# Infini-attention and a tanhshrink feed-forward on one core: a third tile of P and of row maxima, beta planned instead of issued by hand, and a margin on the latencies of the planner

## The chip, the cores and the metric

The kernel runs on one core of a Trainium2 chip. Its time is the device time of one execution in microseconds, and smaller is better. A core has five engines that run side by side, each through its own list of instructions in order: PE (TensorE, the matrix array, whose weight loads are listed as PEld), DVE (VectorE), ACT (ScalarE), POOL (GpSimd) and SP (SyncE, which here only issues DMA transfers). They wait for one another by semaphores. PSUM is the memory that PE writes to, in banks; SBUF is the memory that all engines share.

## The reference

The first half is attention with a compressive memory, over 8 batches, 8 heads, 576 positions and 64 dimensions; the second is a feed-forward block on its 4608 x 512 result:

```
scores = q k^T / 8, causal;  a = softmax(scores);  local = a v
q_p = phi(q),  phi(x) = where(x > 0, x, exp(x) - 1) + 1
mem_out = (q_p M_prev) / (q_p . z_prev + 1e-6)
g = 1 / (1 + exp(-beta))                       # one number per head
x = g * mem_out + (1 - g) * local
out = (h - tanh(h)) @ w_out,  h = x @ w_in     # 512 -> 2048 -> 512
```

All inputs are float32; the kernel reads the two weight matrices as pairs of 32-bit words and decodes them on DVE.

## The kernel before

**Stages.** Attention goes head by head, 64 steps t (lines 1052 to 1121). In step t the scores of head t are made while the probabilities of head t - 1 are transposed and multiplied by V. Beside it, as work that fills PE, runs the first part of the feed-forward block, 6 of the 16 column chunks of `w_in` (`feed_a`, lines 1212 to 1241; its PSUM tiles are `psM`). When attention has been planned to its end, its memory is given back (line 1397), and the remaining 10 chunks are decoded into it and multiplied (`feed_b`, lines 1243 to 1384; PSUM tiles `psB`).

**One head.** `scores` (lines 900 to 939) multiplies q^T by k^T into a PSUM tile (`psS`, two banks, or `psA`), in three groups for the four query chunks. For each chunk DVE adds the causal mask, scales, writes the result into the SBUF tile `P` and the negated row maximum into `nm` (`masked`, line 333), and ACT takes the exponential in place and the row's sum (line 235). `P` and `nm` come from rings, lines 665 and 667: two tiles each before the change, given out in turn, so that head t + 2 writes where head t was. `scale_phi` (lines 941 to 960) takes 1 + exp(beta) (`eb`) into the row's sum and puts the memory's part of the row into `P` as well. `transp` (lines 962 to 981) transposes `P` on PE, and ACT and DVE copy the result to `pt` (for the first 6 head pairs to other tiles, `t` and `g`). `pv` (lines 989 to 1020) multiplies by V. The first 6 pairs (`EPV`, line 22) use plain float32 matmuls, the others a split into a rounded high part and the rest (`qx`, `kx`, `kz`, `vs`).

**Phi.** `prep_phi` (lines 807 to 822) makes phi(q) from q in natural layout (`qn`): two activations on ACT, a vector operation to `ph`, a product with `z` on POOL or DVE, a sum, and then `nr`, for which `enbx` = 1 + exp(-beta) is read (line 819).

**Before the plan.** Some instructions are issued by hand, in the order in which they stand (lines 703 to 734): the loads of the first pair's q^T on SP's queue and k^T on ACT's, the load of `beta` on ACT's queue (line 710), the mask and the identity on POOL, the copies of the mask and two exponentials of beta on ACT (lines 718 to 721), and on DVE four small instructions that make `eb`, `enbx` and `ebp` (lines 722 to 729). On ACT and DVE they so stand ahead of all planned work.

**The planner.** Everything else goes through `Plan` (line 104). A call like `pl.act` only notes an operation with its cost in ns, its engines and what it reads and writes. `run` (line 365) then simulates the engines: at each moment a free engine takes, among the operations that are ready, the one with the best rank. An operation is ready when those that it depends on have ended and `LAT` of their engine has passed (line 27; lines 458, 541 and 548); a PSUM bank is free `LAT` after its last user. A DMA's result counts as there 2000 ns after its end. From a first pass by priorities (`pl.pri`) follow four in all, each ranked by how late the pass before could have done an operation (`_latest`, line 402), so by the length of what hangs on it; the best is kept (lines 372 to 378). Then the instructions are given to each engine in the order of the plan. Engines start in it at the times of `START` (line 31). On the chip only the order counts; the engines wait for real semaphores.

**Fill.** To keep PE at work early, 44 matmuls on a tile of zeros (`zb`, line 738) stand at its head. Up to 60 us of planned time a gap in PE's plan is filled with more (line 384): gap less 60 ns, over 66 ns.

Of the kernel before, what the change touches and what calls it, by code (L numbers as in the profile page):

```python
# [9 lines left out]
F32 = mybir.dt.float32  # L10
# [3 lines left out]
AF = mybir.ActivationFunctionType  # L14
ALU = mybir.AluOpType
# [8 lines left out]
FCA = 6  # L24
PASSES = 4

LAT = {"PE": 200.0, "ACT": 150.0, "DVE": 130.0, "POOL": 150.0, "SP": 250.0}
FIRST = 44
FILL = 60e3

# [73 lines left out]
class Plan:  # L104
# [297 lines left out]
    def _latest(self, order):  # L402
# [33 lines left out]
        while left:  # L436
# [3 lines left out]
            for e in self.ENGINES:  # L440
                if free[e] <= now and heaps[e]:
# [13 lines left out]
                    for j in before[i]:  # L455
                        same = e == "PE" and eng[j] == "PE"
                        ready[j] = max(
                            ready[j], end + ops[j]["tail"] + (0.0 if same else LAT[eng[j]]))
                        need[j] -= 1
# [8 lines left out]
    def _schedule(self, todo, until, rank):  # L468
# [9 lines left out]
        for i in todo:  # L478
            d = [j for j in ops[i]["deps"] if ops[j]["end"] is None]
            need[i] = len(d)  # L480
            ready_at[i] = max(
                [ops[j]["end"] + LAT["SP"] for j in ops[i]["deps"] if ops[j]["end"] is not None],
                default=0.0,
# [10 lines left out]
        while len(done) < len(todo) and (until is None or left):  # L494
# [11 lines left out]
            for e in self.ENGINES:  # L506
# [4 lines left out]
                while h:  # L511
# [29 lines left out]
                    for x, pl in places:  # L541
                        x.left -= 1
                        if not x.left:
                            pl.user, pl.since = None, end + LAT[e]
                            heapq.heappush(wake, pl.since)
                    for j in succ.get(i, ()):
                        same = e == "PE" and ops[j]["opts"][0][0] == "PE"
                        ready_at[j] = max(ready_at[j], op["end"] + (0.0 if same else LAT[e]))
                        need[j] -= 1
# [19 lines left out]
def kernel(  # L569
# [11 lines left out]
    nc = tc.nc  # L581
# [3 lines left out]
    HP = H // 2  # L585
# [23 lines left out]
    att = att_ctx.enter_context(tc.tile_pool(name="att", bufs=1))  # L609
    ps_a = att_ctx.enter_context(tc.tile_pool(name="ps_a", bufs=1, space=PSUM))  # L610

    pl = Plan(nc)
# [14 lines left out]
    ident = const.tile([128, 128], F32, name="ident")  # L627
    mask = const.tile([128, S], F32, name="mask")
    mask0 = const.tile([128, HP, 64], F32, name="mask0")
    eb = const.tile([128, H], F32, name="eb")  # L630
    enb = const.tile([128, H], F32, name="enb")
    ebp = const.tile([128, HP], F32, name="ebp")
    enbx = const.tile([128, HP, 5, 2], F32, name="enbx")
    bt = const.tile([128, H], F32, name="bt")
# [27 lines left out]
    c0t = att.tile([128, HP, 128], F32, name="c0t")  # L662
    r_n0 = Ring(att, "n0", [128, 2, HP], F32, 2)
    r_xT = Ring(att, "xT", [128, 512], F32, 2)
    r_P = Ring(att, "P", [128, 1792], F32, 2)

    r_nm = Ring(att, "nm", [128, 12], F32, 2)
    r_rs = Ring(att, "rs", [128, 2, 4], F32, 2)
    rd = [dram.tile([2, 512], F32, name=f"rd{n}") for n in range(2)]
    r_tmp = Ring(att, "tmp", [128, 640], F32, 1)  # L670
# [35 lines left out]
    for h in range(2):  # L706
        a = slice(64 * h, 64 * h + 64)
        for w, e in ((0, nc.sync), (1, nc.scalar)):
            e.dma_start(out=r_qk.t[0][a, w], in_=qk[0, 0, a, w, h])
    nc.scalar.dma_start(out=bt, in_=beta.partition_broadcast(128))  # L710
    nc.gpsimd.memset(mask, 0.0)
    mf = mask[:, S - 128:S]
    nc.gpsimd.affine_select(
        out=mf, in_=mf, pattern=[[-1, 128]], compare_op=ALU.is_ge,
# [2 lines left out]
    make_identity(nc, ident)  # L717
    for a in (slice(0, 64), slice(64, 128)):
        nc.scalar.copy(mask0[a], mf[a, a].unsqueeze(1).broadcast_to([64, HP, 64]))
    nc.scalar.activation(out=eb, in_=bt, func=AF.Exp)  # L720
    nc.scalar.activation(out=enb, in_=bt, func=AF.Exp, scale=-1.0)
    nc.vector.tensor_scalar(
        out=eb, in0=eb, scalar1=1.0, scalar2=1e20, op0=ALU.add, op1=ALU.min)
    nc.vector.tensor_scalar(
        out=enbx, in0=enb.rearrange("p (a h) -> p a h", h=2).unsqueeze(2).broadcast_to(
            [128, HP, 5, 2]),
        scalar1=1.0, scalar2=None, op0=ALU.add)
    nc.vector.tensor_copy(ebp[0:64, :], eb[0:64, 0::2])
    nc.vector.tensor_copy(ebp[64:128, :], eb[64:128, 1::2])
    nc.gpsimd.memset(c0q, 0.0)  # L730
    for i in range(2):
        nc.gpsimd.memset(r_kz.t[i].bitcast(F32), 0.0)
    for t in (ident, mask, mask0, eb, ebp, enbx):
        pl.const.add(t.tensor.name)


# [21 lines left out]
    def load_qn(pr):  # L758
        b, p = divmod(pr, HP)
        d = prs.setdefault(pr, {})  # L760
        d["qn"] = r_qn.next()
        pl.dma(d["qn"], qn[b, p], False)
        zt[pr] = r_z.next()
        pl.dma(
            zt[pr], z_prev[b, 2 * p:2 * p + 2].rearrange("h d -> (h d)").partition_broadcast(128),
            False,
        )

    def load_qk(pr, w):
        b, p = divmod(pr, HP)  # L770
        d = prs.setdefault(pr, {})
        if pr < EPV:
            t = r_qk.next()
            d["qx"], d["kx"] = t[:, 0, 64:S], t[:, 1]
            for h in range(2 if pr else 0):
                a = slice(64 * h, 64 * h + 64)
                pl.dma(t[a], qk[b, p, a, :, h], False)
        else:
            d["raw"] = r_qk.next()
            pl.dma(d["raw"], qk[b, p, :, w], False)  # L780

    def load_v(pr):
        b, p = divmod(pr, HP)
        d = prs.setdefault(pr, {})
        if pr < EPV and (EPV - pr) % 2:
            d["vm"] = r_tmp.t[0].rearrange("p (c h d) -> p c h d", c=5, h=2)
        else:
            d["vm"] = r_vm.next()
        pl.dma(d["vm"], vm[b, p], False)
# [17 lines left out]
    def prep_phi(pr):  # L807
        p = pr % HP
        x = prs[pr]["qn"]
        e, ph, nr = r_e.next(), r_ph.next(), r_nr.next()  # L810
        pl.act(e, x, AF.Relu, scale=-1.0)
        pl.act(e, e, AF.Exp, scale=-1.0)
        pl.stt(ph, x, 0.0, e, ALU.max, ALU.add)
        pl.tt(
            e.rearrange("p c h d -> p c (h d)"), ph.rearrange("p c h d -> p c (h d)"),
            zt[pr].unsqueeze(1).broadcast_to([128, 5, 2 * D]), ALU.mult, "PV",
        )
        pl.red(nr, e, ALU.add)
        pl.stt(nr, nr, 1e-6, enbx[:, p], ALU.add, ALU.mult)
        pl.recip(nr, nr)  # L820
        d = prs.setdefault(pr, {})
        d["ph"], d["nr"] = ph, nr

    def prep_q(pr):
        d = prs.setdefault(pr, {})
        load_qk(pr, 0)
        if pr < EPV:
            return
        raw = d["raw"][:, :, 64:S]
        qx = d["qx"] = r_qx.next()  # L830
        pl.copy(qx, raw, "PAV")
        lo = slice(64, 128)
        pl.tt(qx[lo], raw[lo], qx[lo].bitcast(F32), ALU.subtract, "PV")
# [217 lines left out]

    def attention():
        pl.pri = -2.0
        prep_q(0)
        load_qn(0)
        pl.pri = 0.0
        prep_phi(0)
        load_v(0)
        load_c0(0)
        c0_phi(0)  # L1060
        load_qn(1)
        for t in range(2 * NPR + 1):
            pl.pri = float(t)
            pr, h = divmod(t, 2)
            act = t < 2 * NPR
            prv = t >= 1
            nxt = pr + 1 < NPR

            def at(key, f, *args):
                pl.pri = t + SH[key]  # L1070
                f(*args)

            order = ORD[h]
            if act:
                at('S', scores, t, order[0])
            if prv:
                at('T', transp, t - 1, 1)
                at('T', transp, t - 1, 2)
            if act:
                at('S', scores, t, order[1])  # L1080
                if h == 0 and pr % HP == HP - 1:
                    at('C', c0_trans, pr // HP)
            if prv:
                at('V', pv, t - 1, (1,))
                at('T', transp, t - 1, 3)
                at('V', pv, t - 1, (2,))
            if act:
                if h == 0 and pr % HP == HP - 1:
                    at('C', c0_out, pr // HP)
                at('S', scores, t, order[2])  # L1090
                at('N', scale_phi, t)
                if h:
                    at('N', turn_rs, pr)
            if prv:
                at('T', transp, t - 1, 0)
            if act and nxt:
                if h == 0:
                    at('P', prep_phi, pr + 1)
                    at('P', c0_phi, pr + 1)
                    at('P', prep_q, pr + 1)  # L1100
                else:
                    at('P', prep_k, pr + 1)
                    if pr + 2 < NPR:
                        at('L', load_qn, pr + 2)
            if prv:
                at('V', pv, t - 1, (3, 4, 0))
                if h == 0:
                    at('V', scale_x, pr - 1)
                    at('V', store_x, pr - 1)
            if act and nxt and h == 0:  # L1110
                if pr < EPV:
                    at('L', load_v, pr + 1)
                if pr + 1 >= EPV:
                    at('P', prep_v, pr + 1)
                    if pr + 2 < NPR:
                        at('L', load_v, pr + 2)
            if act and nxt and h == 1:
                if pr % HP == HP - 2:
                    at('C', c0_scores, pr // HP)
                if pr % HP == HP - 1:  # L1120
                    at('L', load_c0, pr // HP + 1)
# [366 lines left out]
```

## Time and profile before

| | us |
|---|---|
| three runs | 1195.31, 1202.38, 1201.07 |
| their median | 1201.07 |
| the profiled execution | 1203.01 |
| its span, first to last instruction | 1201.2 |
| mean granted TensorE clock in it | 0.989 |
| PE idle in the span (1201.2 - 1176.1) | 25.1 |

The profile is that of one execution. A busy PE is not PE at its peak, since matmuls overlap and their ends are modelled. The granted clock is the share of full speed that the chip let TensorE have. A wait is put down to the instruction that came last. Rows of a timeline give start, duration, engine, line, operation, tile written and tile read; "SPq" and "ACTq" mark the issue of a DMA transfer, not the transfer.

### The profile page before, as it was taken

To read this page: it belongs to the slowest core of one execution; us is meant where nothing else is said; L and a number is where in the kernel's file an instruction comes from. 1 tells how busy PE (TensorE), PEld (TensorE's weight loads), DVE (VectorE), ACT (ScalarE), POOL (GpSimd) and SP (SyncE) were. 2 spreads that over 40 slices of the span, in tenths; PEclk is the share of its full clock that TensorE was granted. 3 is DMA by queue.
4 is the path that set the end of the run, shared out by engine and by line. 5 is a ranking of instruction groups with operands and counts; after the bars stand their busy time and mean duration, and the time that the engine had idled before them with its cause. 6 is when DMAs were issued, how large, how long until landed. Compare 5 with 4: busy or idle time off the path is not lost. (4 is left out here: it accounts for less than half of the span.)

```text
span 1201.2 us, 20181 instructions
## 1 busy us (share of the span) xinstructions
PE 1176.1 (98%) x6899; PEld 1008.8 (84%) x6899; DVE 892.4 (74%) x2103; ACT 691.9 (58%) x1590; POOL 527.6 (44%) x580
## 2 busy tenths in 40 slices
PE   8999989999999999999999999999999999999998
PEld 4455878888898889889888888899898989889897
DVE  3767998898888887888875999893755739375571
ACT  4778986888788768777774565441322415142230
POOL 3566777888778866777670122020101102010110
PEclk7999999999999999999999999999999999999999
DMA  5566455455446354554412454312213031221101
GB/s 144 163 179 184 143 168 209 153 188 153 158 141 213 124 196 124 178 164 141 146 40 106 158 187 147 93 56 81 69 38 88 19 92 34 86 63 45 52 20 53
DMA packets 89831, 143.93 MB, mean 120 GB/s; under 512 B 20736, under 2 KB 54784, under 8 KB 89728
## 3 DMA queue, kind: packets, MB, share of 16 engines
q1 hardware_dynamic: 89424, 142.34, 37.9%
q8 instruction: 54, 0.88, 0.3%
q10 hardware_dynamic: 304, 0.30, 0.1%
q14 instruction: 49, 0.40, 0.1%
HBM read 114.17 MB, written 28.44 MB: 119 GB/s over the span
## 5 line engine op out<-in xcount | busy, mean ns | idle before, releaser
L203 PE MATMUL psB<-wi,ws 128*128 128x256 f32 x1620 | 210.1, 283 | 0.9 <-DVE t L271 0.7
L203 PEld LDWEIGHTS psB<-wi,ws 128*128 128x128 f32 x1620 | 203.9, 191 | 5.3 <-DVE ot L271 1.2
L203 PE MATMUL psM<-xh,wi 128*128 128x384 f32 x576 | 166.6, 349 | 1.8 <-DVE g L271 1.7
L235 ACT ACTIVATE P<-P,nm 128x576 f32<-128x576 f32 (+3 forms) x256 | 157.2, 617 | 19.4 <-DVE nm L333 18.5
L203 PE MATMUL psB<-woB,wo 128*128 128x512 f32 x612 | 148.9, 390 | 0.0
L211 PE MATMUL psA<-ident,P 128*128 128x128 f32 x886 | 143.6, 278 | 1.8 <-DVE pt L271 1.8
L203 PE MATMUL psM<-wo,gh 128*128 128x512 f32 x432 | 145.4, 402 | 0.0
L211 PEld LDWEIGHTS psA<-ident,P 128*128 128x128 f32 x886 | 106.8, 142 | 39.9 <-issue 11.5
L271 DVE TENSOR_TENSOR pt<-psA,pt 128x512 fp32r<-128x512 f32 (+1 forms) x208 | 124.9, 616 | 20.5 <-ACT pt L247 18.9
L271 DVE TENSOR_TENSOR ot<-psB,ot 128x256 f32<-128x256 f32 x225 | 87.7, 419 | 70.5 <-ACT ot L247 55.5
L203 PE MATMUL psA<-pt,vs 128*128 128x512 f32 (+3 forms) x520 | 129.8, 351 | 6.3 <-DVE pt L271 4.5
L203 PEld LDWEIGHTS psB<-woB,wo 128*128 128x128 f32 x612 | 112.8, 188 | 22.0 <-DVE wo L271 0.2
L247 ACT CAST pt<-psA 128x512 fp32r<-128x512 f32 (+1 forms) x208 | 107.5, 532 | 40.4 <-PE psA L211 38.2
L203 PEld LDWEIGHTS psM<-xh,wi 128*128 128x128 f32 x576 | 105.2, 190 | 6.3 <-DVE g L271 3.4
L203 PEld LDWEIGHTS psA<-pt,vs 128*128 128x128 f32 x520 | 87.6, 193 | 16.7 <-DVE pt L271 6.1
L203 PE MATMUL psM<-xl,wi 128*128 128x384 f32 x288 | 99.4, 345 | 0.0
L247 ACT COPY ot<-psB 128x256 f32<-128x256 f32 x22 | 8.2, 374 | 154.6 <-PE psB L203 153.4
L276 POOL TENSOR_TENSOR P<-ph,nm 128x128 f32<-128x128 f32 x128 | 67.2, 544 | 62.7 <-DVE nm L271 30.7
L203 PEld LDWEIGHTS psM<-wo,gh 128*128 128x128 f32 x432 | 79.1, 188 | 13.1 <-DVE g L271 0.3
L271 DVE TENSOR_TENSOR rawB<-psB,xh 128x512 f32<-128x512 f32 x34 | 23.3, 689 | 88.5 <-PE psB L203 88.4
L333 DVE CUSTOM_DVE_ANT_0 P<-psA,mask 128x320 f32<-128x320 f32 (+2 forms) x160 | 69.5, 458 | 25.7 <-PE psA L203 20.1
L333 DVE CUSTOM_DVE_ANT_0 P<-psS,mask 128x576 f32<-128x576 f32 (+1 forms) x96 | 67.8, 706 | 26.0 <-PE psS L203 21.0
(226 smaller groups left out, 2619.3 us busy)
## 6 DMA issues: line engine op xcount, KB each, us to landing
qk<-in_qk_dram SPq DMA_DIRECT2D x52, 576.0 KB
qn<-in_qn_dram SPq DMA_DIRECT2D x32, 320.0 KB
vm<-in_vm_dram SPq DMA_DIRECT2D x29, 320.0 KB
xh<-part SPq DMA_DIRECT2D x36, 256.0 KB
out_dram<-rawB SPq DMA_DIRECT2D x36, 256.0 KB
xr<-xs SPq DMA_DIRECT2D x11, 768.0 KB
part<-ot SPq DMA_DIRECT2D x11, 768.0 KB
e<-rd SPq DMA_DIRECT2D x64, 128.0 KB
```

The source lines that it names most:

```text
L203: [("PE", max(109.0, n * c / 2.4 + 13), lambda: nc.tensor.matmul(real(out), lhsT, rhs, start=start, stop=stop, **kw))],
L211: [("PE", self._n(out) * 2 / 2.4 + 3, lambda: nc.tensor.transpose(real(out), in_, ident))],
L235: [("ACT", c, lambda: nc.scalar.activation(out=out, in_=real(in_), func=func, **kw))],
L247: "ACT", n / 1.2 + (51 if ps else 93), lambda: nc.scalar.copy(out, real(in_))
L271: lambda: nc.vector.tensor_tensor(out=out, in0=real(a), in1=b, op=op),
L276: lambda: nc.gpsimd.tensor_tensor(out=out, in0=a, in1=b, op=op),
L333: [("DVE", self._n(out) / 0.96 + 115, lambda: nc.vector.tensor_tensor_reduce(out=real(out), in0=real(in_), in1=mask, scale=-scale, scalar= ...
```

## The change

Three parts. The rings of P and of row maxima get a third tile each. The load of beta moves from ACT's queue to SP's and becomes a planned operation, the first that is noted, with the priority of the first loads of q (-2); the two exponentials and four DVE instructions on it are planned too, and `eb`, `enbx` and `ebp` are marked as constant after that. And `LAT` rises by 200 ns for PE, ACT, DVE and POOL; SP's stays.

```diff
-LAT = {"PE": 200.0, "ACT": 150.0, "DVE": 130.0, "POOL": 150.0, "SP": 250.0}
+LAT = {"PE": 400.0, "ACT": 350.0, "DVE": 330.0, "POOL": 350.0, "SP": 250.0}
...
-    r_P = Ring(att, "P", [128, 1792], F32, 2)
-
-    r_nm = Ring(att, "nm", [128, 12], F32, 2)
+    r_P = Ring(att, "P", [128, 1792], F32, 3)
+
+    r_nm = Ring(att, "nm", [128, 12], F32, 3)
...
-    nc.scalar.dma_start(out=bt, in_=beta.partition_broadcast(128))
...
-    nc.scalar.activation(out=eb, in_=bt, func=AF.Exp)
-    nc.scalar.activation(out=enb, in_=bt, func=AF.Exp, scale=-1.0)
-    nc.vector.tensor_scalar(
-        out=eb, in0=eb, scalar1=1.0, scalar2=1e20, op0=ALU.add, op1=ALU.min)
-    nc.vector.tensor_scalar(
-        out=enbx, in0=enb.rearrange("p (a h) -> p a h", h=2).unsqueeze(2).broadcast_to(
-            [128, HP, 5, 2]),
-        scalar1=1.0, scalar2=None, op0=ALU.add)
-    nc.vector.tensor_copy(ebp[0:64, :], eb[0:64, 0::2])
-    nc.vector.tensor_copy(ebp[64:128, :], eb[64:128, 1::2])
...
-    for t in (ident, mask, mask0, eb, ebp, enbx):
+    for t in (ident, mask, mask0):
         pl.const.add(t.tensor.name)
...
     def attention():
         pl.pri = -2.0
+        pl.dma(bt, beta.partition_broadcast(128), False)
+        pl.act(eb, bt, AF.Exp)
+        pl.act(enb, bt, AF.Exp, scale=-1.0)
+        pl.ts(eb, eb, 1.0, 1e20, ALU.add, ALU.min)
+        pl.ts(
+            enbx, enb.rearrange("p (a h) -> p a h", h=2).unsqueeze(2).broadcast_to([128, HP, 5, 2]),
+            1.0, None, ALU.add, None)
+        pl.copy(ebp[0:64, :], eb[0:64, 0::2], "V")
+        pl.copy(ebp[64:128, :], eb[64:128, 1::2], "V")
+        for t in (eb, ebp, enbx):
+            pl.const.add(t.tensor.name)
         prep_q(0)
         load_qn(0)
```

## The prediction

> **What bounds the kernel now.** I read the page first, then the stretches table (busy time of each engine by stage), then the opening in order of time, then the waits of attention.
>
> ```profile
> span 1201.2 us, 20181 instructions
> PE 1176.1 (98%) x6899; PEld 1008.8 (84%) x6899; DVE 892.4 (74%) x2103; ACT 691.9 (58%) x1590; POOL 527.6 (44%) x580
> ```
>
> TensorE has work in 1176.1 of 1201.2 us. The profiled execution took 1203.0 us with its span of 1201.2, so 1.8 lie outside. What the change can win is idle time of PE, 25.1 us, and what a lower granted clock costs. The stretches table says where both lie (columns: stretch, its length, PE, PEld, DVE, ACT, POOL busy with counts, granted clock, DMA share, GB/s):
>
> ```profile
> 0.00:8.30 8.30, 7.32 (x53) 6.37 (x54) 0.11 (x1) 2.09 (x3) 4.19 (x11) 1.00 0.56 131
> 8.30:10.40 2.10, 0.03 (x1) 0.06 (x1) 0.00 (x0) 0.00 (x0) 0.00 (x0) 0.91 0.58 189
> 10.40:12.30 1.90, 0.00 (x0) 0.00 (x0) 1.34 (x7) 1.60 (x5) 0.00 (x0) 0.50 0.82 297
> 12.30:27.50 15.20, 15.19 (x34) 6.71 (x33) 8.62 (x29) 7.96 (x22) 3.41 (x5) 0.51 0.52 132
> 30.00:120.00 90.00, 90.00 (x368) 45.34 (x368) 62.26 (x173) 70.01 (x170) 55.56 (x63) 1.00 0.60 175
> 120.00:630.00 510.00, 495.90 (x3013) 439.78 (x3012) 433.50 (x1053) 403.97 (x960) 389.86 (x421) 0.99 0.49 155
> 630.00:720.00 90.00, 88.56 (x453) 78.68 (x453) 76.59 (x165) 50.80 (x107) 13.57 (x9) 1.00 0.45 150
> 750.00:1201.20 451.20, 447.46 (x2781) 404.45 (x2779) 279.00 (x619) 138.28 (x294) 51.02 (x66) 1.00 0.20 59
> ```
>
> Three places. The opening: PE empty from 8.3 to 12.3 us, then half clock until 27.5. Attention proper, 120 to 630: 510.0 - 495.9 = 14.1 us idle, and a clock of 0.99. The end from 750 on is full but for 3.7 us, most of it the drain of the last block, which no part of the change touches. So the second half is not where I look for a gain.
>
> The opening in order of time (start, duration, engine, line, what; in brackets the idle time before and its releaser):
>
> ```profile
> 0.98 4.98 PE L738 MATMUL psS<-zb 128*128 128x128 bf16 x45 [0.98 <-DVE zb L704]
> 1.99 0.58 SPq L348 DMA_DIRECT2D qn<-in_qn_dram  x1
> 2.25 0.62 ACTq L710 DMA_DIRECT2D bt<-in_beta_dram  x1
> 2.62 0.43 SPq L348 DMA_DIRECT2D z<-in_z_prev_dram  x1
> 5.89 1.57 PE L203 MATMUL psS<-qk 64*128 64x288 f32 x4
> 10.67 0.21 ACT L720 ACTIVATE eb<-bt 128x8 f32<-128x8 f32 x1 [5.66 <-DMA bt<-in_beta_dram]
> 10.89 0.72 ACT L235 ACTIVATE e<-qn 128x640 f32<-128x640 f32 x1
> 10.91 0.17 DVE L722 TENSOR_SCALAR eb<-eb 128x8 f32<-128x8 f32 x1 [9.98 <-ACT eb L720]
> 11.49 0.76 DVE L333 CUSTOM_DVE_ANT_0 P<-psS,mask 128x576 f32<-128x576 f32 x1
> 12.29 0.78 ACT L235 ACTIVATE P<-P,nm 128x576 f32<-128x576 f32 x1
> 12.31 0.27 PE L738 MATMUL psS<-zb 128*128 128x128 bf16 x1 [3.98 <-DVE nm L333]
> 14.51 2.07 PE L203 MATMUL psA<-qk 64*128 64x192 f32 x4
> 15.29 0.67 ACT L235 ACTIVATE P<-P,nm 128x448 f32<-128x448 f32 x1 [1.14 <-DVE nm L333]
> 16.52 0.69 PE L211 MATMUL psA<-ident,P 128*128 128x128 f32 x2
> ```
>
> Beta's 4 KB land at 10.67, 8.4 us after their issue. ACT and DVE run in order, and both have what is made of beta at their heads. The first scores are in PSUM at 5.89 + 1.57 = 7.46, but DVE's first masked maximum starts at 11.49, because four small instructions on beta stand before it. PE needs that PSUM bank again and waits 3.98 us.
>
> **The change, part by part.** Durations are from rows; the planner's own costs I use for the order of work alone.
>
> (1) Beta. Gone from the head: ACT's DMA issue (0.62), two exponentials (0.21 for the first) and four DVE instructions (10.91 to 11.49, 0.58 together). All come back as planned work, so nothing is saved by their removal, only by their place. The first masked maximum is then free at about 7.5 instead of 11.49. The next PE instruction followed that start by 12.31 - 11.49 = 0.82, so it comes at 8.3, and the 3.98 us gap closes. The issue moves to SP. The planner's ranks put first what has the longest chain behind it: q's natural tile feeds two 640-wide activations and three wide vector operations before it meets what beta gives, which has one 8-wide activation and one small vector operation; so I expect q first and beta second or third. z, the first weight block and V, behind it, are issued up to 0.62 later; z is first read by POOL after a 640-wide vector operation that hasn't begun at 12.31, so that is covered; uncovered it would be 0.62. Beta will hardly land before 10. What stands behind it on ACT is then the exponential of the first scores (12.29 now), on DVE the fourth masked maximum, no longer the first. Late next, in that order: q's tile for ACT, and head 0's exponentials, for which PE's first transposes (16.52) wait.
>
> What that is worth. If q lands only just before 10.89, the first exponential of scores stays at 12.29, but the last of the four no longer waits 1.14 for a PE slowed behind the gap: transposes about 1.4 earlier. At best the whole gap is won on top, 1.4 + 4.0 = 5.4, because head 1's scores (2.07 us and more, after 14.51) fit into the wait. I take 3.5, about the middle, and keep 0 to 5.4, 0 for the case that beta lands later than now.
>
> The half clock from 10.4 to 27.5 is a second price: 15.2 us of PE work at about 0.51 would be 7.6 shorter at full clock. I don't take it. The rows of attention say why:
>
> ```profile
> 190.94:194.35 3.41, 1.76 (x8) 0.87 (x6) 3.31 (x7) 3.38 (x9) 3.41 (x5) 1.00 0.28 43
> 194.35:197.77 3.42, 3.42 (x11) 2.93 (x12) 2.88 (x8) 1.69 (x7) 2.08 (x3) 0.50 0.88 362
> 324.06:327.47 3.41, 1.37 (x9) 1.11 (x7) 3.35 (x4) 0.85 (x2) 3.41 (x3) 1.00 0.52 159
> 327.47:330.90 3.43, 3.43 (x13) 2.96 (x14) 3.31 (x10) 1.99 (x5) 1.95 (x2) 0.50 0.62 183
> 443.40:446.77 3.37, 1.57 (x9) 1.22 (x9) 3.34 (x6) 0.72 (x2) 0.63 (x1) 1.00 0.30 76
> 446.77:450.20 3.43, 3.43 (x13) 3.19 (x12) 1.39 (x7) 0.85 (x3) 3.10 (x6) 0.52 0.52 175
> ```
>
> Three times a stretch of 3.4 us in which PE was busy 1.4 to 1.8 us was followed by one at half clock. In the new opening PE has the rest of head 0's scores and head 1's to do between 8.3 and about 12, then waits for exponentials until about 14: again a stretch that is about half busy. So the drop more likely moves than goes.
>
> [...]
>
> (2) The margin of 200 ns on the four compute engines' hops. It adds no instruction but fill matmuls: fills are planned gap less 60, over 66 ns, so before head 0's third score group one becomes about seven. 45 of them took 4.98 us, 0.11 each, so 0.7 us there, in time in which PE else idles; without that cover the same few groups would cost 1 to 2. It lies inside the 0 to 5.4 above. Otherwise it changes the order on every engine: PE is planned to do another head's or the feed-forward's work for 200 ns more before it meets a result. What it can win is in these rows:
>
> ```profile
> PE psA L203 <- DVE pt L271: 4.5, 4, 2.0
> PE psA L211 <- DVE pt L271: 1.8, 5, 0.7
> PE psA L203 <- DVE nm L333: 1.5, 2, 1.2
> DVE P L333 <- PE psA L211: 5.2, 12, 1.0
> L271 DVE TENSOR_TENSOR qx<-qk,qx x16: 1214/1222/3607, 127.7 to 588.5; 64x1024 fp32r<-64x1024 f32 x16
> ```
>
> (From 120 to 630: waits with total us, times, longest; the last row has minimum, median and maximum ns.) PE's waits for `pt` are nine of 0.7 us on average, (4.5 + 1.8) / 9; two or three hops lie between a transpose and the product that needs it, 0.4 to 0.6 us of new slack. So I take half of the 14.1 us, 7.0, and one clock drop of three, 0.5 x 3.42 = 1.7: about 8.5. Ends: all of it, 14.1 + 3 x 1.7 = 19; and a loss, since a new order also places new collisions: three more stalls like those above (1.6 to 2.0 idle and 1.7 of clock) cost about 11, which the lost order of (3) below rounds to 12.
>
> (3) Third tiles of P and of row maxima. They remove DVE's wait for the transposes that free P, the 5.2 us in 12 above. DVE has 510.0 - 433.5 = 76.5 us idle there, so alone this is worth nothing on the path; it lets the margin's earlier scores start. They cost only memory. Cover gone, it is at most 5.2.
>
> Sum: 1203.0 - 3.5 - 8.5 = **1191.0**. The median of the three runs, 1201.07, is 1.9 below the profiled execution and the runs spread over 7; I make no correction and count the difference into the range.
>
> **The rivals.**
>
> *The opening keeps its clock.* If the fills and head 1's scores keep PE more than about half busy until the transposes, the 7.6 come on top: 1203.0 - 3.5 - 7.6 - 8.5 = **1183.4**. For it: six fills more per gap, a gap of 4 us less. Against it: the three pairs of rows above.
>
> *The margin is too small for what it meets.* The three drops coincide with DVE subtractions of `qx` that took up to 3.607 us against a median of 1.222; 2.4 us is not met by 0.2 per hop. Then attention stays and only the opening counts: 1203.0 - 3.5 = **1199.5**. For it: long stalls hold much of the 14.1. Against it: most waits for `pt` are shorter than 1 us. [...]
>
> *Attention becomes longer than its cover (slower).* Larger latencies make the planner slip a feed-forward matmul in front of attention work that is in truth ready. One per head, at 15.0 / 81 = 0.185 us (row below), over 64 heads is 11.8. Attention then ends 11.8 later, and so begins the decoding of the second half's weights, which needs attention's memory and fills DVE:
>
> ```profile
> 690.00:705.00 15.00, 15.00 (x81) 14.04 (x80) 15.00 (x35) 9.30 (x20) 0.00 (x0) 1.00 0.48 160
> ```
>
> The matmuls that cover it between 630 and 720 were spent early, so PE idles that long: 1203.0 - 3.5 + 11.8 = **1211.3**. It decides as soon as the matmuls left at attention's end last less than the decoding, and now they end about when it does: PE 88.56 of 90 from 630 to 720. Against it: only if PE's extra matmuls delay attention and don't fill its 14.1 idle.
>
> **How the numbers follow.** Forecast 0.38, kept clock 0.24, margin too small 0.25, slower attention 0.13. About 1% (12 us: below 1189 or above 1213) is what a measurement of this kernel tells from no change. Faster by more: nine tenths of the kept clock (0.22), four tenths of the forecast (0.15), little else: 0.38. Slower by more: half of the last rival, whose 1211.3 is near the border (0.07), and a bad end of the attention term otherwise (0.03): 0.10. Within: 0.52. The range must reach the kept clock at 1183.4 with some of the attention term's upper half, and the third rival with a few lost microseconds, and leave out most of the last: 1179 to 1208.
>
> **What would show it.** Right: the first masked maximum at about 7.5, beta's issue on SP behind q's natural tile, no PE gap of 4 us before 12; PE idle from 120 to 630 near 7 and two drops instead of three; the wait of masked maxima for transposes all but gone. The half clock beginning one or two stretches later, at 13.8 or 17, is the forecast; none before 30 is the first rival. Wrong: idle of 14 or more in attention with the qx maximum unchanged (margin too small), or psM matmuls ended long before the first psB ones, with PE idle between (slower).

## The result and the profile after

The changed kernel takes 1177.26 us (median of four runs, 1175.71 to 1178.65); the kernel before took 1198.57 beside it (four runs, 1195.31 to 1202.38). The ratio is 0.9838, with a 95% interval of 0.98 to 0.9876. The forecast of 1191.0 had the direction and, against 1201.07, half of the size (0.8% of 1.6%); the time in us lies 1.7 below the low end of its range, 1179 (as a share, 1179 of 1201.07 is 0.9816, and the measured ratio lies above it). The profiled execution took 1178.65, its span is 1176.8.

First the stretches table of the changed kernel:

```profile
8.30:10.40 2.10, 2.10 (x14) 1.24 (x13) 1.88 (x7) 1.69 (x6) 0.00 (x0) 1.00 0.91 312
...
12.30:27.50 15.20, 14.94 (x65) 7.39 (x63) 11.52 (x40) 11.32 (x31) 6.29 (x9) 1.00 0.85 191
120.00:630.00 510.00, 500.71 (x3090) 454.61 (x3090) 433.88 (x1051) 404.19 (x961) 385.23 (x419) 1.00 0.51 157
630.00:720.00 90.00, 88.03 (x465) 78.05 (x464) 88.40 (x191) 46.37 (x98) 11.05 (x11) 0.98 0.48 152
```

PE is no longer empty from 8.3 on, and the clock stays full from 12.3 to 27.5, where it was 0.51: 65 matmuls instead of 34. From 120 to 630 PE idles 9.3 us instead of 14.1. The opening in order of time:

```profile
2.24 0.60 SPq L348 DMA_DIRECT2D qn<-in_qn_dram  x1
...
2.88 0.43 SPq L348 DMA_DIRECT2D bt<-in_beta_dram  x1
3.36 0.51 SPq L348 DMA_DIRECT2D z<-in_z_prev_dram  x1
...
6.34 0.74 ACT L235 ACTIVATE e<-qn 128x640 f32<-128x640 f32 x1 [2.27 <-DMA qn<-in_qn_dram]
...
7.11 0.21 ACT L235 ACTIVATE enb<-bt 128x8 f32<-128x8 f32 x1
...
7.34 0.76 DVE L333 CUSTOM_DVE_ANT_0 P<-psS,mask 128x576 f32<-128x576 f32 x1 [6.41 <-PE psS L203]
...
8.14 0.78 ACT L235 ACTIVATE P<-P,nm 128x576 f32<-128x576 f32 x1
...
8.64 1.02 PE L203 MATMUL psS<-qk 64*128 64x448 f32 x2
...
8.88 0.82 DVE L315 SCALAR_TENSOR_TENSOR ph<-qn,e 128x640 f32<-128x640 f32 x1
...
10.52 1.55 POOL L276 TENSOR_TENSOR e<-ph,z 128x640 f32<-128x640 f32 x1 [5.66 <-DMA z<-in_z_prev_dram]
...
10.86 0.44 PE L211 MATMUL psA<-ident,P 128*128 128x128 f32 x2
```

Beta is second in SP's queue, behind q's natural tile. Both had landed when ACT could use them, q at 6.34 and beta by 7.11 (no bracket, so no wait). The first masked maximum starts at 7.34, and the first transposes at 10.86, 5.7 us earlier than before.

To see where the time came from, I cut each profiled execution at two starts: the last product of the six early head pairs with V out of `t` (the PE row below), and the last sum into `xT`, which ends attention (the DVE row). Rows by tile give them (minimum, median, maximum ns; first and last start). Before:

```profile
L271 DVE TENSOR_TENSOR xT<-psA,tmp x52: 621/689/696, 148.3 to 644.0; 64x512 f32<-64x512 f32 x52
L203 PE MATMUL psA<-t,tmp x24: 592/592/644, 42.9 to 132.7; 128*64 128x512 f32 x24
```

After:

```profile
L271 DVE TENSOR_TENSOR xT<-psA,tmp x52: 621/690/696, 134.0 to 619.6; 64x512 f32<-64x512 f32 x52
L203 PE MATMUL psA<-t,tmp x24: 592/593/643, 36.2 to 122.8; 128*64 128x512 f32 x24
```

So the early pairs end at 122.8 instead of 132.7 (9.9 less), attention from there takes 619.6 - 122.8 = 496.8 instead of 511.3 (14.5 less), and the rest 1176.8 - 619.6 = 557.2, as before (1201.2 - 644.0 = 557.2). Together 24.4, the difference of the spans. The medians differ by 21.3: the profiled execution lies 4.4 above the median before and 1.4 after.

The stretches table of the middle part alone, before and after:

```profile
132.70:644.00 511.30, 497.77 (x3022) 443.06 (x3021) 427.22 (x1037) 399.21 (x949) 382.14 (x414) 0.99 0.48 152
```

```profile
122.80:619.60 496.80, 487.51 (x3017) 442.56 (x3016) 424.66 (x1029) 398.62 (x948) 382.11 (x416) 1.00 0.50 155
```

Only 4.2 of the 14.5 are idle time of PE (511.3 - 497.8 = 13.5 became 9.3). The other 10.3 lie in its busy time, with almost the same number of matmuls. Some 3.4 of these are clock, by my estimate, since two stretches of 3.4 us at half clock are gone (0.50 from 402.0 to 405.4 is the one left; before there were three, at 0.50, 0.50 and 0.52); about 6.9 are time in which PE reads as busy at full clock on the same work.

### The profile page after: what moved, and what is told of

Its sections match the earlier page's. It is cut to its first block, busy times and chain, and to the rows that moved or that the text cites. A ratio compares the mean times of both kernels' runs of the same rounds, so it can differ in the third digit from the quotient of the medians.

```text
span 1176.8 us, 20151 instructions
## 1 busy us (share of the span) xinstructions
PE 1160.3 (99%) x6907; PEld 1005.3 (85%) x6907; DVE 904.3 (77%) x2133; ACT 673.4 (57%) x1565; POOL 516.2 (44%) x575
## 5 line engine op out<-in xcount | busy, mean ns | idle before, releaser
L203 PE MATMUL psB<-wi,ws 128*128 128x256 f32 x1620 | 212.5, 284 | 2.0 <-DVE ot L271 1.6
L235 ACT ACTIVATE P<-P,nm 128x320 f32<-128x320 f32 (+3 forms) x256 | 156.8, 615 | 9.6 <-DVE nm L333 8.8
L203 PE MATMUL psB<-woB,wo 128*128 128x512 f32 x612 | 153.3, 391 | 0.0
L211 PE MATMUL psA<-ident,P 128*128 128x128 f32 x883 | 140.6, 276 | 6.3 <-DVE pt L271 5.2
L247 ACT COPY ot<-psB 128x256 f32<-128x256 f32 x44 | 16.4, 372 | 148.8 <-PE psB L203 143.0
L203 PE MATMUL psM<-wo,gl 128*128 128x512 f32 x216 | 86.3, 402 | 0.0
L276 POOL TENSOR_TENSOR P<-ph,nm 128x128 f32<-128x128 f32 x128 | 63.9, 518 | 45.1 <-DVE nm L271 29.7
```

The source lines that it names most:

```text
L203: [("PE", max(109.0, n * c / 2.4 + 13), lambda: nc.tensor.matmul(real(out), lhsT, rhs, start=start, stop=stop, **kw))],
L211: [("PE", self._n(out) * 2 / 2.4 + 3, lambda: nc.tensor.transpose(real(out), in_, ident))],
L235: [("ACT", c, lambda: nc.scalar.activation(out=out, in_=real(in_), func=func, **kw))],
L247: "ACT", n / 1.2 + (51 if ps else 93), lambda: nc.scalar.copy(out, real(in_))
L276: lambda: nc.gpsimd.tensor_tensor(out=out, in0=a, in1=b, op=op),
```

## The experiments

My theory after the result: beta's place gives the early part, by an earlier start and by the clock; the margin gives attention; the third tile gives nothing by itself. Rivals: the clock is kept by the fill that the margin plans; the margin needs the third tile; the shorter attention is only the luck of a new order. The third tiles with the old latencies have no plan at all (the planner comes to a point where nothing is ready and nothing ends), so "without margin" beside three tiles is a margin of 10 ns.

The cuts of all profiled executions, by the same two rows, and the times with their ratio to the kernel before, run beside them ("PE busy" is PE's busy time within attention). Each cut is of one execution: e5's took 1198.3, where its median is 1203.4.

| kernel | early pairs | attention | PE busy | rest | median | ratio (interval) |
|---|---|---|---|---|---|---|
| before | 132.7 | 511.3 | 497.8 | 557.2 | 1198.6 | |
| changed | 122.8 | 496.8 | 487.5 | 557.2 | 1177.3 | 0.9838 (0.98 to 0.9876) |
| e1 beta | 121.9 | 508.7 | 497.0 | 557.5 | 1190.2 | 0.9915 (0.9895 to 0.9936) |
| e2 margin | 136.1 | 497.8 | 488.1 | 562.0 | 1196.1 | 0.9959 (0.993 to 0.9988) |
| e3 tiles | 130.2 | 504.4 | 494.6 | 559.8 | 1194.5 | 0.9943 (0.9921 to 0.9965) |
| e4 fill | 131.4 | 508.1 | 494.7 | 557.4 | 1197.3 | 0.9969 (0.9946 to 0.9991) |
| e5 margin, tiles | 129.1 | 506.7 | 488.8 | 560.7 | 1203.4 | 1.0023 (1.0002 to 1.0043) |
| e6 beta, margin | 126.7 | 503.0 | 487.5 | 561.9 | 1195.5 | 0.9974 (0.9956 to 0.9993) |
| e7 beta, tiles | 124.3 | 509.9 | 495.6 | 560.3 | 1192.4 | 0.9936 (0.9914 to 0.9957) |
| e8 fill, other bank | 125.4 | 508.4 | 494.8 | 556.9 | 1192.3 | 0.9932 (0.9915 to 0.9949) |
| e9 190 ns | 122.0 | 494.5 | 487.2 | 559.6 | 1180.5 | 0.9851 (0.9825 to 0.9877) |
| e10 210 ns | 127.0 | 503.9 | 488.7 | 554.4 | 1185.1 | 0.9886 (0.9851 to 0.992) |
| e11 300 ns | 122.6 | 495.0 | 487.5 | 559.2 | 1178.1 | 0.9825 (0.9808 to 0.9843) |
| e12 100 ns | 121.5 | 507.2 | 490.5 | 557.1 | 1190.9 | 0.9932 (0.9909 to 0.9956) |

**e1, beta alone.**

```diff
 # the changed kernel, with
+LAT = {"PE": 200.0, "ACT": 150.0, "DVE": 130.0, "POOL": 150.0, "SP": 250.0}
+    r_P = Ring(att, "P", [128, 1792], F32, 2)
+    r_nm = Ring(att, "nm", [128, 12], F32, 2)
```

> Beta planned, with two tiles of P and the old latencies. If the opening's gain is beta's place alone: first masked maximum near 7.4 us, no PE gap of 4 us, full clock from 7 to 27, and 11 us less than the kernel before, about 1188, with attention as uneven as before (idle from 120 to 630 near 14 us). If the opening keeps its clock only because the margin plans more fill: the half clock comes back at 10 to 17 us, and the time is only about 4 us less, 1195.

The first branch, with 9.3 us less. Its stretches:

```profile
8.30:10.40 2.10, 1.99 (x9) 0.98 (x9) 2.10 (x9) 2.10 (x8) 0.00 (x0) 1.00 0.86 281
...
12.30:27.50 15.20, 15.07 (x62) 6.96 (x61) 12.41 (x38) 11.78 (x29) 6.13 (x9) 1.00 0.74 178
120.00:630.00 510.00, 498.30 (x3038) 444.99 (x3037) 427.06 (x1046) 398.06 (x958) 395.38 (x421) 0.99 0.49 153
```

The clock is full without the margin's fill, so the fill isn't what keeps it here. Attention is nearly as long as before (508.7), with 11.7 us of PE's time idle from 120 to 630.

The clock isn't safe in every execution, though. In e7 (below), also with beta planned and without the margin's fill, beta landed later, and DVE had to make `enbx` of it ahead of head 0's next masked maximum, for which PE waited. The stretch that follows (clock 0.78) lost, by my estimate, about 0.22 x 15.2 = 3.3 us:

```profile
9.29 0.21 ACT L235 ACTIVATE enb<-bt 128x8 f32<-128x8 f32 x1 [2.04 <-DMA bt<-in_beta_dram]
...
9.54 0.18 DVE L291 TENSOR_SCALAR enbx<-enb 128x40 f32<-128x40 f32 x1 [1.27 <-ACT enb L235]
9.63 0.35 DVE L333 CUSTOM_DVE_ANT_0 P<-psA,mask 128x192 f32<-128x192 f32 x1
...
10.46 1.13 PE L203 MATMUL psA<-qk 64*128 64x192 f32 x4 [0.76 <-DVE nm L333]
```

```profile
12.30:27.50 15.20, 15.20 (x48) 6.57 (x47) 9.38 (x32) 10.14 (x28) 4.15 (x8) 0.78 0.62 155
```

The other seven traces with beta planned, e1's among them, read 1.00 there. Whether the margin's fill would have saved e7's is open.

**e2, the margin alone.** Only the line of `LAT` is the changed kernel's.

> The margin alone: beta at the head as before, two tiles of P. If margin and beta are worth their own stretch each: opening as before (gap near 4 us, half clock for about 17), attention 13 us shorter, about 1186. If the margin needs the third tile of P, since heads planned further apart run into the ring: attention no shorter than before, 1199 or more. If the gain in attention is only the luck of a new order: anything from 1190 to 1205.

Attention is 13.5 shorter (497.8 of 511.3), as the first branch said and without a third tile. The time is not: the early part is 3.4 longer than before (136.1), and behind attention 4.8 us are given back (rest 562.0). There, from 630 to 760, PE waits for DVE's sums out of `psB`, a wait that the kernel before doesn't have:

```profile
PE psB L203 <- DVE ot L271: 4.2, 4, 2.4
```

Its ten runs differ by 14 us, and the granted clock goes with them; five of the ten:

```
us        1185.41  1187.15  1194.11  1196.26  1199.76
clock       1.000    0.997    0.991    0.988    0.989
```

By its clock of 0.989 I estimate that the slowest run lost 0.011 x 1199.76 = 13.2 us; the run at full clock is 14.4 faster.

**e3, the third tiles alone**, the kernel before with three tiles and 10 ns.

> The third tiles alone, with a margin of 10 ns instead of 200. If the ring is off the path: within 4 us of the kernel before, 1195 to 1203, and the wait of masked maxima for PE's transposes falls. If the ring is what makes attention shorter: about 1186, with idle from 120 to 630 below 10 us.

1194.5, just below the first branch; PE's idle time from 120 to 630, 9.8 us, is that of the second, but not its time. Attention is 6.9 shorter, but the wait of masked maxima for transposes is 4.9 us in 8 where it was 5.2 in 12, so that wait isn't the reason.

**e4 and e8, the kernel before with PE kept at work.** e4 puts 76 matmuls on zeros where one stood, e8 72 into another bank:

```diff
+                if pe is not None and n and not self.filled:
+                    n, self.filled = 0, True
+                    for _ in range(72):
+                        self.idle(other=True)
                 for _ in range(n):
                     self.idle()
...
+    def idle(first=False, other=False):
+        to = bM[1].tile[:, 0:128] if other else bS[0].tile[:, 832:960]
+        nc.tensor.matmul(to, zb, zb, start=first or other, stop=False, skip_group_check=True)
```

> The kernel before with 76 matmuls on zeros instead of one behind the first scores, where PE waits for beta; beta stays where it is. If the half clock that follows is what the wait costs most: full clock up to 27 us and beyond, about 7 us less, 1191, though DVE begins no earlier than 11.5. If the cost is the late start itself: no less than 2 us are won, 1197 or more.

e4 missed its own point. The zeros go to the tile whose scores wait for DVE, so they wait too, and then stand in the way:

```profile
11.54 6.47 PE L741 MATMUL psS<-zb 128*128 128x128 bf16 x76 [3.63 <-DVE nm L334]
```

> The kernel before, with 72 matmuls on zeros into a PSUM bank that nothing else uses at that time, behind the first scores, where PE waits for beta; beta stays at the head. PE is then busy from 8.3 to about 12.3. If PE's idle time is what halves the clock, and the clock lost is time lost one for one: clock share near 0.997 instead of 0.992, 6 to 7 us less than before, about 1193. If the clock falls for another reason (little work in the matmuls of the first heads): half clock from 13 on all the same and within 2 us of before.

e8 does fill the wait, and 7.4 us are won:

```profile
8.30:10.40 2.10, 2.10 (x42) 2.10 (x40) 1.81 (x9) 1.11 (x4) 0.00 (x0) 1.00 1.00 334
...
12.30:27.50 15.20, 15.20 (x64) 7.29 (x62) 11.67 (x35) 11.87 (x31) 6.66 (x9) 1.00 0.54 140
```

The same work on beta at the head, and a full clock: the early pairs end 7.3 earlier (125.4). Beta landed earlier as well, at 8.30 instead of 10.67. But PE's next scores, which here stand behind the zeros, start only 0.5 earlier than in the kernel before (first row e8, second row before), so about 6.8 of the 7.3 are clock:

```profile
11.99 1.02 PE L204 MATMUL psS<-qk 64*128 64x448 f32 x2
```

```profile
12.51 1.86 PE L203 MATMUL psS<-qk 64*128 64x448 f32 x2
```

e1, where DVE also starts earlier (7.79 instead of 9.12), has 121.9. The 3.5 between them are that start or the other order; one pair can't tell. In the kernel before, the half clock lasted through 15.2 us in which PE reads as busy (0.51 from 12.3 to 27.5), where a drop in attention was one stretch (0.50 from 194.35 to 197.77), by my estimate 0.5 x 3.42 = 1.7 us; for the opening the two traces say about 6.8.

**e5, e6, e7: one part taken back.** e5 has beta at the head again, e6 two tiles, e7 a margin of 10 ns.

> The changed kernel with beta's load, exponentials and vector instructions back at the head: margin and third tiles alone. If each part is worth its own stretch: opening with a gap of 2 to 4 us and a half clock of 17 us, attention as short as in the changed kernel; about 10 us over it, 1187 to 1189. If margin and third tile are worth only what each alone was (3.4 and 5.0 of 1199.5): 1191. If a third tile is what the margin needs: clearly less than 1191.

> The changed kernel with two tiles of P and of row maxima: beta and margin alone. If the parts add up: 1199.5 less 9.3 for beta and 3.4 for the margin, 1187. If the margin needs the third tile: no better than beta alone, 1190 or more. If the ring is off the path: 1177, as the changed kernel.

> The changed kernel with a margin of 10 ns in place of 200: beta and third tiles alone. If the parts add up: 1199.5 less 9.3 for beta and 5.0 for the tiles, 1185. If the margin is what shortens attention: 1190, as beta alone. If any new order is as good as the margin: 1177 to 1180.

e6 and e7 went their middle branches in time: each is no better than beta alone, so the parts do not add up run by run. e5 missed all of its figures. Its ten runs have clocks from 0.988 to 0.994, so part of its 1203 is clock; and PE idles 17.9 us in its attention (506.7 - 488.8), more than in the kernel before. Why, no run shows. In the cuts the three lie between the kernel before and the changed one: attention 506.7 and 503.0 with the margin, 509.9 without.

**e9 to e12: other margins**, 190, 210, 300 and 100 ns in the changed kernel.

> The changed kernel with a margin of 190 ns instead of 200. If the margin as such shortens attention: within 2 us of the changed kernel, 1175 to 1179, and nearly its order. If the order that came out of 200 is a lucky one among many: another order, attention 3 to 12 us longer, 1180 to 1192.

> The same with 210 ns. Margin as such: 1175 to 1179. Lucky order: 1180 to 1192, and not the same time as with 190.

> The same with 300 ns. If more slack goes on helping: 1177 or less. If the slack is paid for where weights of the second half are decoded (margin and third tiles alone had PE idle there): 630 to 750 us with PE below 116 of 120 and 1182 or more. Lucky order: 1180 to 1192.

> The same with 100 ns. If the margin works by its size: between no margin (1192.4 with 10 ns) and the changed kernel (1177.3), about 1185. Lucky order: no relation, anything from 1177 to 1195.

Ten ns less or more make another order, with 494.5 and 503.9 us of attention: so there is luck, about 5 us to either side. But it has a centre. The seven kernels with 190 ns or more have 494.5 to 506.7, 499.7 in the mean; the four orders with 10 ns or none have 504.4 to 511.3, 508.6 in the mean (e4 and e8 have the order of before). The margin is worth 8.9 us there, in the mean.

PE's busy time in attention shows it more clearly, for it doesn't overlap: 487.2 to 488.8 in the seven with 190 ns or more, 494.6 to 497.8 in the four with 10 ns or none, with 3001 to 3035 matmuls in all of them. That is 8.3 of the 8.9. Clock alone doesn't make it: e7 and e9 both read a clock of 1.00 from 120 to 630, and have 495.6 and 487.2. PE's idle time, attention less busy time, does overlap, 7.3 to 17.9 and 9.8 to 14.3: that is where one order differs from another. With 100 ns attention is as long as without a margin (507.2), but PE's busy time, 490.5, has already fallen most of the way, and 16.7 us of idle time hide it.

Two tiles or three make no difference that stands out: 497.8 and 503.0 with two and the margin. e11 came between its first two branches: no more is won with 300, and PE is busy 116.6 of 120 us from 630 to 750. The waits there show best in e9:

```profile
690.00:705.00 15.00, 9.62 (x60) 9.05 (x60) 14.51 (x29) 5.46 (x12) 10.98 (x3) 0.84 0.52 157
```

```profile
700.46 0.68 DVE L315 SCALAR_TENSOR_TENSOR mask<-rawB,mask 128x512 int32<-128x512 int32 x1
701.06 0.41 DVE L252 COPY ot<-psB 128x256 f32<-128x256 f32 x1
701.40 1.07 DVE L271 TENSOR_TENSOR ot<-psB,ot 128x256 f32<-128x256 f32 x3
...
701.95 2.90 PE L203 MATMUL psB<-wi,ws 128*128 128x256 f32 x12 [5.38 <-DVE ot L271]
```

PE has 5.4 us idle and loses clock (0.84), while DVE is busy 14.51 of 15 us. PE waits for sums that DVE takes out of `psB`, and they stand in DVE's order behind the decoding of weights (`rawB`). That attention's earlier end (616.5, 27.5 us before that of the kernel before) puts the decoding there is likely, but not shown.

No kernel beats the changed one beyond the noise: e11 has the lowest ratio, and its interval overlaps the changed kernel's.

## Why the prediction was half right

*What bounds the kernel*: right. All of the gain lies before attention's end; the rest is 557.2 in both.

*(1) Beta, the earlier start, 3.5*: one pair agrees in size (e1 against e8: 3.5), but the eight orders with beta planned differ by 5.5 among themselves (121.5 to 127.0), so that isn't shown. The order in SP's queue, q, beta, z, was right.

*(1) The clock*: the step that failed. I priced it at 7.6 and didn't take it, since "the drop more likely moves than goes". It is about 6.8 in e8, and it went. Under that sentence stood two wrong landings: "Beta will hardly land before 10", and q's natural tile put as late as 10.89. They came by 7.11 and at 6.34, so the first transposes started at 10.86 and not at about 14, and the half-busy stretch that I laid out between never came. What the forecast feared does exist: e7, where beta landed at 9.29, lost 3.3 us of clock. The rival that keeps its clock named what came (1.00 from 12.3 to 27.5), and its 1183.4 is the nearest of the four figures; of its two reasons the gap mattered, and the fills were not needed in e1.

*(1) What is displaced*: z held POOL up, but only from the end of `ph` at 8.88 + 0.82 = 9.70 to 10.52, 0.8 us; the 5.66 in its row are all of POOL's idle time. No PE wait follows from it, so that cover held.

*(2) The margin, 8.5*: near the mean over orders (8.9), too small for this order (14.5), and near the mean by luck. I took 7.0 from PE's idle time and 1.7 from the clock, and put its busy time at nothing. In the changed kernel idle time gave 4.2, the clock 3.4 and the rest of the busy time 6.9; in the mean, idle time gave 0.6 and busy time 8.3. PE's own waits for `pt` did not shrink: 4.5 + 1.8 in nine became 5.2 + 1.4 in five. What went are its waits for row maxima, of which the matmuls' view has no row left (1.5 on `psA` and 1.3 on `psS` before), and most waits of the weight loads, which run beside the matmuls. Theirs before, from 120 to 630 (total us, times, longest):

```profile
PEld psA L203 <- DVE pt L271: 6.2, 7, 2.3
...
PEld psA L203 <- DVE nm L333: 2.4, 3, 1.6
PEld psS L203 <- DVE nm L333: 2.3, 4, 1.8
```

The same view of the changed kernel:

```profile
PEld psA L203 <- DVE pt L271: 1.6, 1, 1.6
...
PEld psA L203 <- DVE nm L333: 0.2, 1, 0.2
```

and its matmuls' waits for `pt`:

```profile
PE psA L211 <- DVE pt L271: 5.2, 4, 2.1
...
PE psA L203 <- DVE pt L271: 1.4, 1, 1.4
```

The products' loads for `pt` go from 6.2 to 1.6 and those for row maxima from 4.7 to 0.2. All rows of that view add up to 33.7 us in 72 waits before and 16.2 in 23 after; over the kernels it is 53 to 72 waits without the margin and 23 to 46 with it. Many short waits gone, a few long ones left: that fits a slack of 200 ns. That these waits are the busy time that went is argued, not shown. The rival "too small" saw its cause rightly: the one half clock left in attention, at 402 us, follows a subtraction of `qx` that took 2.55 us and a wait of PE of 2.11 us, and by the rows by tile another still takes 3.711; why some take that long, no run shows:

```profile
L271 DVE TENSOR_TENSOR qx<-qk,qx x13: 1222/1224/3711, 131.2 to 565.4; 64x1024 fp32r<-64x1024 f32 x13
```

But most of what could be won lay elsewhere. The clock fell once in attention instead of three times; I had taken one drop gone.

*(3) The tiles, nothing alone*: not refuted, though e3 is 5 us faster than before; 504.4 of attention is within what a new order does. That their wait would be all but gone was wrong: from 120 to 630 it is

```profile
DVE P L333 <- PE psA L211: 4.3, 7, 1.4
```

after 5.2 in 12. What they do bring in one order or another stays open: two tiles and three can't be planned in the same order.

*The slower rival* asked for attention longer than its cover. Attention became shorter, and PE still came to wait beside the decoding: 1.6 us at 699 in the changed kernel, 5.4 in e9, each time for DVE's sums out of `psB`. That is a place to look at next.

In sum, beta's place is worth 8.4 in the early part (mean of eight kernels with it, 123.6, against four with it at the head and no added fill, 132.0) and the margin 8.9 in attention: 17.3 of the 24.4. Of the other 7, 3.4 are what the profiled execution of the kernel before lies above these means, and 3.7 what that of the changed one lies below: order and execution, which can't be told apart here.

Whole times say less. At equal tiles the kernel with the margin is 3.4 us faster (e2 against 1199.5 before) and 15.1 (changed against e7), but 5.3 slower (e6 against e1) and 8.9 slower (e5 against e3); in e2, e5 and e6 the rest is 3.5 to 4.8 longer than before, which eats part of what attention gives. With beta planned and three tiles, all four margins from 190 to 300 are 7 to 15 us faster than e7. So a part for the third tile in the whole time, beside the margin, isn't ruled out.

## What to carry to other kernels

A small transfer whose result stands at the head of an in-order engine can cost more than the wait itself: here PE's wait of 4.0 us was followed by about 6.8 us lost to a half clock (e8 against the kernel before). Look at the granted clock behind each gap, and price the gap and the clock apart. A planner that schedules to the last nanosecond gained here from slack of 200 ns, but one order is one draw, here worth 5 us to either side. Try neighbours before crediting a parameter, and compare busy time on the same work beside the total: here it separated the kernels with the margin from those without, where the total didn't.

## What was not expected of the hardware

The landing of beta's 4 KB differs widely between the traces of kernels that issue it from ACT's queue at about 2 us. The latest and the earliest with beta at the head, e3 and e5:

```profile
11.21 0.21 ACT L720 ACTIVATE eb<-bt 128x8 f32<-128x8 f32 x1 [6.20 <-DMA bt<-in_beta_dram]
```

```profile
7.15 0.21 ACT L720 ACTIVATE eb<-bt 128x8 f32<-128x8 f32 x1 [2.43 <-DMA bt<-in_beta_dram]
```

It is 8.30 in e8, 8.94 in e2, 9.90 in e4 and 10.67 before. PE's wait goes with it: 5.06 us in e3, 3.98 before, 2.30 in e2, 1.56 in e5. The half clock behind it doesn't: it lasts to 26 us in e3 and 27 before, but to 30 in e2 and 21 in e5 (clock from 12.3 to 27.5: 0.55, 0.51, 0.50 and 0.70), although PE reads as busy from the wait's end on (in e2 and e5 for all 15.20 us from 12.3 to 27.5). In e2:

```profile
27.50:30.40 2.90, 2.90 (x8) 1.36 (x8) 2.90 (x8) 0.00 (x0) 0.86 (x1) 0.50 0.00 0
```

e4, whose PE worked on zeros from 11.54 to 18.0, had its clock back at 15.9:

```profile
12.50:15.93 3.43, 3.43 (x35) 3.43 (x33) 0.42 (x1) 0.88 (x4) 1.54 (x1) 0.50 0.58 179
15.93:27.50 11.57, 11.57 (x80) 7.16 (x78) 6.90 (x23) 6.25 (x16) 1.88 (x4) 1.00 0.40 98
```

Whether what PE works on makes that difference, and not only whether it reads as busy, no run isolates. The landings may be why runs of e2 spread over 14 us and those of the changed kernel over 3, but only one execution of each kernel has a trace, so that isn't shown.
